# Probabilities as the stationary operand of probability x V, with a ones column in V, in a fused attention and SwiGLU kernel

## The chip, the cores and the metric

The kernel runs on one core of a Trainium2 chip. The metric is the device time of one execution in microseconds (us). Before the change it is 379.1 us (median of 4 runs, 378.8 to 379.4). In these runs the time is always 1.7 us more than the span from the first to the last instruction that a profile shows.

## The reference, cut to what matters

```python
B, H, S, D = 4, 8, 768, 64            # attention; d_ff = 1536, d_model = H * D = 512
scores = q @ k.T / sqrt(D)            # per batch and head
scores = where(mask, scores, -1e9)    # block mask of 32x32 blocks
attn = exp(scores - max);  attn = attn / (sum(attn) + 1e-9)
x = (attn @ v) with the heads side by side        # (B*S, 512)
xn = x / sqrt(mean(x * x) + 1e-6) * rms_g
out = (silu(xn @ w_gate) * (xn @ w_val)) @ w_out  # (3072, 512), float32
```

## The kernel before

The program counts in *units* of 384 tokens (half a batch; 8 of them) and in *head pairs* (4 per unit, 32 in all). A software pipeline has 192 steps; each step does the scores of one pair for 128 keys (two matmuls) and their exp on ScalarE. The probability x V of a pair, the norm of a unit and the feed-forward of the unit before are placed between the steps by a fixed list and a work queue. Scores come out with keys on partitions, so the probabilities `pt` are already laid out as either operand of the product with V.

Before the change V is the stationary operand and the probabilities stream through. The two heads of a pair use the two 64-column halves of the array at the same time (in the trace the second head's matmul starts 3 to 4 ns after the first's). The result has head and value dimension on partitions, as the feed-forward wants it. The row sums of the probabilities need matmuls of their own, in four 32-column parts of the array:

```python
def av(n, shared):
    ...
    for jt in range(NC):                       # NC = 6 blocks of 128 keys
        for e in range(2):                     # two heads
            nc.tensor.matmul(
                out=o_[64 * e:64 * e + 64, :],
                lhsT=vb[:, 2 * pr + e, jt * D:(jt + 1) * D],
                rhs=pt_[:, jt, e, :], start=(jt == 0), stop=(jt == NC - 1), ...)
    nc.vector.tensor_copy(out=osb[u][:, pr, :], in_=o_)
    nc.gpsimd.tensor_tensor(                   # squares for the norm
        out=o2s[u][:, pr, :], in0=osb[u][:, pr, :], in1=osb[u][:, pr, :], op=ALU.mult)

def zsum(n):                                   # row sums: 12 matmuls of 32 x 384
    ...
                    nc.tensor.matmul(
                        out=zwt[u][32 * c:32 * c + 32, :], lhsT=Ez[:, pr, :],
                        rhs=pt_[:, 2 * j2 + par, e, :], ...)
# norm_a ... norm_e (cut): sums and sums of squares are gathered by selection matmuls,
# turned by fp32 matmuls, combined on VectorE, turned back, and broadcast to 128
# partitions by matmuls; VectorE multiplies them into osb to make xn.
...
LAG = 13                                       # steps from a unit's scores to its feed-forward
    at(s1 + 1, 1.2, av, n, n >= 8)
    at(s1 + 1, 0.7, zsum, n)
    if pr == NP - 1:
        at(s1 + 4, 0.4, norm_a, u)  ...  at(s1 + 12, 0.35, norm_e, u, 1)
```

`at(step, cost, function, ...)` puts a function at a step; `s1` is the first step after a pair's scores.

The softmax here doesn't subtract the row's maximum and nothing guards it: scores larger than these inputs give would overflow.

Of the kernel before, what the change touches and what calls it, by code (L numbers as in the profile page):

```python
# [17 lines left out]
def kernel(  # L18
# [12 lines left out]
    nc = tc.nc  # L31
# [34 lines left out]
    qraw, kraw, vtiles = {}, {}, {}  # L66
# [8 lines left out]
    def load_v(b):  # L75
        vtiles[b] = vpool.tile([P, H, NC * D], BF16, name="vb", tag="vb")
        nc.gpsimd.dma_start(out=vtiles[b], in_=vv[b])
# [6 lines left out]
    gcol = const.tile([P, DM // P], FP32, name="gcol")  # L84
    nc.sync.dma_start(out=gcol, in_=moe_rms_g.rearrange("(c p) -> p c", p=P))
# [95 lines left out]
    for ic in range(2):  # L181
        qm = ps_a.tile([32, TG], FP32, name="qm", tag="zw" if ic else "acc")
        nc.tensor.matmul(
            out=qm, lhsT=Bneg[0:NB, :],
            rhs=Kindf[0:NB, ic * TG:(ic + 1) * TG], start=True, stop=True)
        nc.scalar.copy(
            out=Xm[:, 0:2, 0, ic * TG:(ic + 1) * TG],
            in_=qm.unsqueeze(1).to_broadcast([32, 2, TG]))

    def mask_rows(lo, hi):  # L190
# [7 lines left out]
    Ez = const.tile([P, NP, 32], BF16, name="Ez")  # L198
    nc.gpsimd.memset(Ez, 0.0)
    nc.gpsimd.affine_select(  # L200
        out=Ez, in_=Ez, compare_op=ALU.not_equal, fill=1.0,
        base=0, pattern=[[1, NP], [-1, 32]], channel_multiplier=0)
    Ew = const.tile([P, 32], BF16, name="Ew")
    nc.gpsimd.memset(Ew, 0.0)
    for e in range(2):
        nc.gpsimd.memset(Ew[64 * e:64 * e + 64, 16 + e:17 + e], 1.0)

    Sel = const.tile([P, 16], FP32, name="Sel")
    nc.gpsimd.memset(Sel, 0.0)
    for half in range(2):  # L210
        nc.gpsimd.affine_select(
            out=Sel[:, 0:8], in_=Sel[:, 0:8], compare_op=ALU.not_equal, fill=1.0,
            base=-32 * half, pattern=[[-1, NP], [-64, 2]], channel_multiplier=1)
    nc.gpsimd.affine_select(
        out=Sel[:, 8:16], in_=Sel[:, 8:16], compare_op=ALU.not_equal, fill=1.0,
        base=-16, pattern=[[-32, NP], [-1, 2]], channel_multiplier=1)

    SelB = const.tile([P, NP, 2, D], BF16, name="SelB")
    nc.gpsimd.memset(SelB, 0.0)
    for half in range(2):  # L220
        nc.gpsimd.affine_select(
            out=SelB, in_=SelB, compare_op=ALU.not_equal, fill=1.0,
            base=-32 * half, pattern=[[-2, NP], [-1, 2], [0, D]], channel_multiplier=1)
    FHL = [const.tile([P, NT, P], BF16, name=f"FHL{i}") for i in range(2)]
    for t in FHL:
        nc.gpsimd.memset(t, 0.0)
# [5 lines left out]
    ptiles, osb, zwt, xns, hps, o2s = {}, {}, {}, {}, {}, {}  # L232
# [16 lines left out]
    def av(n, shared):  # L249
        u, pr = divmod(n, NP)  # L250
        b = u // 2
        pt_, vb = ptiles[n], vtiles[b]
        if pr == 0:
            osb[u] = opool.tile([P, NP, TG], FP32, name="osb", tag="osb")
            o2s[u] = work.tile([P, NP, TG], BF16, name="o2", tag="o2")
            zwt[u] = ps_a.tile([P, 512], FP32, name="zw", tag="zw")[:, 0:TG]
        if shared:
            o_ = ps_s.tile([P, 2, 512], FP32, name="o_", tag="s")[:, 0, 0:TG]
        else:
            o_ = ps_a.tile([P, 512], FP32, name="oa", tag="acc")[:, 0:TG]  # L260
        for jt in range(NC):
            for e in range(2):
                nc.tensor.matmul(  # L263
                    out=o_[64 * e:64 * e + 64, :],
                    lhsT=vb[:, 2 * pr + e, jt * D:(jt + 1) * D],
                    rhs=pt_[:, jt, e, :], start=(jt == 0), stop=(jt == NC - 1),
                    skip_group_check=True)
        nc.vector.tensor_copy(out=osb[u][:, pr, :], in_=o_)  # L268
        nc.gpsimd.tensor_tensor(  # L269
            out=o2s[u][:, pr, :], in0=osb[u][:, pr, :], in1=osb[u][:, pr, :], op=ALU.mult)  # L270

    def zsum(n):
        u, pr = divmod(n, NP)
        pt_ = ptiles[n]
        for j2 in range(NC // 2):
            for e in range(2):
                for par in range(2):
                    c = 2 * e + par
                    nc.tensor.matmul(  # L279
                        out=zwt[u][32 * c:32 * c + 32, :], lhsT=Ez[:, pr, :],  # L280
                        rhs=pt_[:, 2 * j2 + par, e, :],
                        start=(pr == 0 and j2 == 0), stop=False, skip_group_check=True)

    nrm = {}

    def norm_a(u):
        for pr in range(NP):
            nc.tensor.matmul(
                out=zwt[u][32 * pr:32 * pr + 32, :], lhsT=Ew, rhs=o2s[u][:, pr, :],
                start=False, stop=True, skip_group_check=True)  # L290
        zs = work.tile([P, TG], FP32, name="zs", tag="zs")
        nc.vector.tensor_copy(out=zs, in_=zwt.pop(u))
        nrm[u] = zs

    def norm_b(u):
        zs = nrm[u]
        zt = ps_a.tile([P, NT, 16], FP32, name="zt", tag="zw")
        for t in range(NT):
            nc.tensor.matmul(
                out=zt[:, t, :], lhsT=zs[:, t * P:(t + 1) * P], rhs=Sel,  # L300
                start=True, stop=True)
        zc = work.tile([P, NT, 16], FP32, name="zc", tag="zc")
        nc.vector.tensor_copy(out=zc, in_=zt)
        rz = work.tile([P, NT, 8], FP32, name="rz", tag="rz")
        nc.vector.reciprocal(out=rz, in_=zc[:, :, 0:8])
        w1 = work.tile([P, NT, 8], FP32, name="w1", tag="w1")
        nc.vector.tensor_tensor(out=w1, in0=zc[:, :, 8:16], in1=rz, op=ALU.mult)
        nc.vector.tensor_tensor(out=w1, in0=w1, in1=rz, op=ALU.mult)
        ms = work.tile([P, NT], FP32, name="ms", tag="ms")
        nc.vector.reduce_sum(out=ms, in_=w1, axis=mybir.AxisListType.X)  # L310
        nc.vector.tensor_scalar(  # L311
            out=ms, in0=ms, scalar1=1.0 / DM, scalar2=1e-6, op0=ALU.mult, op1=ALU.add)
        rs = work.tile([P, NT], FP32, name="rs", tag="rs")
        nc.gpsimd.tensor_tensor(out=rs, in0=ms, in1=nhalf, op=ALU.pow)  # L314
        nrm[u] = (rz, rs)

    def norm_c(u):
        rz, rs = nrm[u]
        fx = work.tile([P, NT, 8], FP32, name="fx", tag="fx")
        nc.vector.tensor_tensor(  # L320
            out=fx, in0=rz, in1=rs.unsqueeze(2).to_broadcast([P, NT, 8]), op=ALU.mult)
        fh = FHL[u % 2]
        nc.vector.tensor_copy(out=fh[:, :, 0:8], in_=fx)
        nc.vector.tensor_tensor(
            out=fh[:, :, 32:40], in0=fx, in1=fh[:, :, 0:8], op=ALU.subtract)

    def norm_d(u):
# [85 lines left out]


    NSTEP = NU * NP * NC
    LAG = 13
    RESERVE = 5
    fixed = {}

# [109 lines left out]
```

## Time and profile before

| | before |
|---|---|
| time, median | 379.1 us |
| TensorE busy / granted clock | 93% / 0.996 |
| ScalarE / VectorE / GpSimd busy | 53% / 55% / 16% |
| first feed-forward matmul | at 52.4 us |
| row sums and probability x V, per pair | 0.60 + 1.10 us, and 0.09 on entering |

The page of the kernel before, part 1 (busy us, share of the span, instructions) and two lines of part 2 (40 slices of the span, each digit a share in tenths):

```profile
PE 352.9 (93%) x2730; PEld 187.9 (49%) x2730; DVE 210.1 (55%) x411; ACT 200.5 (53%) x302; POOL 60.9 (16%) x88
...
PE   2998889988899999999999999999999999999995
...
PEclk9999999999999999999999999999999999999999
```

TensorE is nearly full from the first tenth of the run on. The clock row holds only what was recorded: the first record of the trace is at 22.7 us, so its first 9s say nothing. The other engines have room. The waits of TensorE over the whole run (who waited for whom: us in total, times, longest) are short, and the two longest rows of the list, with one of the single waits, belong to the start or to a few spots:

```profile
PE tqk L165 <- DMA qb<-in_q_dram: 5.0, 1, 5.0
PE ft L332 <- DVE osb L268: 2.3, 3, 1.1
...
PE fb L350 <- ACT pt L246: 0.9, 1, 0.9
```

One head pair in the timeline of TensorE (start, busy us, line, output<-inputs, shape). Busy times of matmuls overlap, so cost is read from one start to the next start:

```profile
190.01 0.49 PE L242 MATMUL s__2404<-X 88*128 88x384 bf16 x2
190.43 1.17 PE L263 MATMUL o__2408<-pt,vb 128*64 128x384 bf16 x12
191.53 0.67 PE L279 MATMUL zw<-pt,Ez 128*32 128x384 bf16 x12
192.13 0.34 PE L242 MATMUL s__2435<-X 88*128 88x384 bf16 x1
```

Probability x V takes 191.53 - 190.43 = 1.10 us, the row sums 192.13 - 191.53 = 0.60 us. The score matmuls ahead of them fill 0.42 us where a pair of them elsewhere takes 0.33 (here 2 x 162 ns): about 0.09 us is lost on entering the 64-column tiling. The Trainium skill says in "TensorEngine Tiling (Array Packing)", Key Properties, that changing the tiling mode drains the array; the trace agrees with about 0.09 us, and the same 0.09 us stand at the other borders of a tiling (32-column sums, 64-column transposes).

### The profile page before, as it was taken

The page shows a single profiled execution, that of the slowest core. Times are in us where ns is not written, and L with a number is a line of the kernel's source. Part 1 is how long each engine was busy: PE and PEld are TensorE (multiplying, and loading weights), DVE is VectorE, ACT ScalarE, POOL GpSimd, SP SyncE. Part 2 cuts the span into 40 slices and gives each one's busy share as a digit, 9 for nine tenths or more (in the row PEclk, how much of TensorE's full clock was granted, in tenths as well). Part 3 has the DMA queues.
Part 4 walks back from the last instruction along what each step waited for, and adds up shares of the span by engine and source line. Part 5 has one row for each costly group of instructions (what it writes and reads, how often), then busy time and mean ns, then how long its engine had stood idle before and what let it go on. Part 6 is the DMA issues. An engine that isn't in the chain of part 4 may idle for free.

```text
span 379.9 us, 6604 instructions
## 1 busy us (share of the span) xinstructions
PE 352.9 (93%) x2730; PEld 187.9 (49%) x2730; DVE 210.1 (55%) x411; ACT 200.5 (53%) x302; POOL 60.9 (16%) x88
## 2 busy tenths in 40 slices
PE   2998889988899999999999999999999999999995
PEld 1443345554555555555555555555555455545552
DVE  5642355666646564665645655565444644676650
ACT  2658566665555555556555555556566566122221
POOL 8970110130010100020010100010000100000000
PEclk9999999999999999999999999999999999999999
DMA  5999970091060000091050000000000000000012
GB/s 70 179 210 207 205 130 2 2 148 19 2 101 11 28 29 2 28 151 45 29 83 29 29 0 29 30 15 14 28 30 0 29 0 29 28 29 28 29 39 99
DMA packets 20257, 20.86 MB, mean 55 GB/s; under 512 B 1284, under 2 KB 17156, under 8 KB 20228
## 3 DMA queue, kind: packets, MB, share of 16 engines
q0 software_dynamic: 16208, 14.16, 24.3%
q1 hardware_dynamic: 4020, 6.30, 4.4%
q8 instruction: 21, 0.34, 0.4%
q14 instruction: 8, 0.07, 0.1%
HBM read 28.31 MB, written 6.29 MB: 91 GB/s over the span
## 4 chain that ended last, share of the span: by engine, by line
PE 76%; DVE 10%; ACT 6%; issue 3%; DMA 2%; POOL 1%; POOLq 0%; DVEq 0%
PE yp L401 14%; PE gp L370 14%; PE vp L387 13%; PE zw L279 5%; ACT pt L246 3%; PE oa L263 3%; ACT th L374 2%; DVE uu L376 2%; DVE xn L355 2%; DVE X L171 2%; PE tqk L165 1%; DVE X L174 1%; DMA kb<-in_k_dram 1%; DMA out_dram<-yo 1%; PE vw L387 1%
## 5 line engine op out<-in xcount | busy, mean ns | idle before, releaser
L376 DVE SCALAR_TENSOR_TENSOR uu<-th,gp 128x384 bf16<-128x384 bf16 x90 | 49.8, 554 | 86.5 <-ACT th L374 86.0
L401 PE MATMUL yp<-wo,hp 128*128 128x512 bf16 x288 | 75.9, 379 | 0.0
L387 PE MATMUL vp<-xn,wv 128*128 128x384 bf16 x360 | 73.2, 325 | 1.3 <-DVE hp L390 1.3
L370 PE MATMUL gp<-xn,wg 128*128 128x384 bf16 x360 | 73.3, 326 | 1.1 <-DVE uu L376 1.1
L374 ACT ACTIVATE th<-gp 128x384 bf16<-128x384 f32 x90 | 44.0, 489 | 50.8 <-PE gp L370 50.8
L242 PEld LDWEIGHTS <-X 88*128 88x128 bf16 x384 | 35.1, 100 | 48.8 <-issue 19.9
L390 DVE TENSOR_TENSOR hp<-uu,vp 128x384 bf16<-128x384 bf16 x90 | 49.8, 553 | 15.9 <-PE vp L387 8.1
L370 PEld LDWEIGHTS <-wg 128*128 128x128 bf16 x384 | 36.6, 97 | 31.8 <-issue 3.3
L387 PEld LDWEIGHTS <-wv 128*128 128x128 bf16 x384 | 36.7, 98 | 26.8 <-issue 2.9
L401 PEld LDWEIGHTS <-hp 128*128 128x128 bf16 x288 | 27.8, 98 | 24.8 <-issue 0.4
L263 PEld LDWEIGHTS <-vb 128*64 128x64 bf16 x384 | 21.1, 112 | 19.1 <-issue 12.7
L174 DVE COPY X<-tqk 64x1536 bf16<-64x1536 bf16 x26 | 24.8, 954 | 5.2 <-PE tqk L165 4.9
L279 PE MATMUL zw<-pt,Ez 128*32 128x384 bf16 x384 | 22.1, 337 | 0.0
L355 DVE SCALAR_TENSOR_TENSOR xn<-osb,gcol,fb 128x384 bf16<-128x384 f32 x28 | 15.9, 609 | 1.7 <-PE fb L350 1.6
L314 POOL TENSOR_TENSOR rs<-ms,nhalf 128x3 f32<-128x3 f32 x8 | 6.9, 866 | 55.8 <-DVE ms L311 55.8
L410 DVE TENSOR_SCALAR yo<-yp 128x512 f32<-128x512 f32 x21 | 14.4, 686 | 0.2
L279 PEld LDWEIGHTS <-Ez 128*32 128x32 bf16 x384 | 7.4, 96 | 12.3 <-issue 10.7
L165 PE MATMUL tqk<-ident,qb 128*64 128x128 bf16 x156 | 7.2, 230 | 5.1 <-DMA qb<-in_q_dram 5.0
L165 PEld LDWEIGHTS <-qb 128*64 128x64 bf16 x192 | 6.7, 120 | 10.3 <-issue 5.3
L263 PE MATMUL oa<-pt,vb 128*64 128x384 bf16 x96 | 11.3, 379 | 0.0
L268 DVE COPY osb<-oa 128x384 f32<-128x384 f32 x8 | 4.5, 557 | 11.3 <-PE oa L263 11.2
L269 POOL TENSOR_TENSOR o_1613<-osb 128x384 bf16<-128x384 f32 x4 | 3.3, 826 | 30.3 <-DVE osb L268 30.3
(557 smaller groups left out, 461.7 us busy)
## 6 DMA issues: line engine op xcount, KB each, us to landing
out_dram<-yo SPq DMA_DIRECT2D x24, 256.0 KB, 2.0
vb<-in_v_dram POOLq DMA_DIRECT2D x4, 768.0 KB, 8.1
qb<-in_q_dram POOLq DMA_DIRECT2D x3, 768.0 KB, 7.4
kb<-in_k_dram POOLq DMA_DIRECT2D x3, 768.0 KB, 11.4
wg<-in_moe_w_gate_dram POOLq DMA_DIRECT2D x2, 768.0 KB, 11.7
wv<-in_moe_w_val_dram POOLq DMA_DIRECT2D x2, 768.0 KB, 14.1
wo<-in_moe_w_out_dram POOLq DMA_DIRECT2D x1, 1536.0 KB, 30.8
qb<-in_q_dram POOLq DMA_DIRECT2D x2, 192.0 KB, 3.6
```

The source lines that it names most:

```text
L165: nc.tensor.transpose(out=tt[i][64 * h:64 * h + 64, c * P:(c + 1) * P], in_=src[:, 2 * pr + h, c * D:(c + 1) * D], identity=ident)
L174: nc.vector.tensor_copy(out=X[0:D, sl, h], in_=t_[64 * h:64 * h + 64, :, 0:S])
L242: nc.tensor.matmul(out=s_[:, e, 0:TG], lhsT=X[0:D + NB, sl, e, 1, jt * P:(jt + 1) * P], rhs=X[0:D + NB, sl, e, 0, ic * TG:(ic + 1) * TG], ...
L263: nc.tensor.matmul(out=o_[64 * e:64 * e + 64, :], lhsT=vb[:, 2 * pr + e, jt * D:(jt + 1) * D], rhs=pt_[:, jt, e, :], start=(jt == 0), stop ...
L279: nc.tensor.matmul(out=zwt[u][32 * c:32 * c + 32, :], lhsT=Ez[:, pr, :], rhs=pt_[:, 2 * j2 + par, e, :], start=(pr == 0 and j2 == 0), stop ...
L355: nc.vector.scalar_tensor_tensor(out=xns[u][:, pr, :], in0=osb[u][:, pr, :], scalar=gcol[:, pr:pr + 1], in1=fb[i], op0=ALU.mult, op1=ALU.mult)
L370: nc.tensor.matmul(out=gp, lhsT=wg[:, c, f * P:(f + 1) * P], rhs=xns[u][:, c, :], start=(c == 0), stop=(c == NP - 1))
L374: nc.scalar.activation(out=th, in_=gp, func=AF.Tanh, scale=0.5)
L376: nc.vector.scalar_tensor_tensor(out=uu, in0=th, scalar=1.0, in1=gp, op0=ALU.add, op1=ALU.mult)
L387: nc.tensor.matmul(out=vp, lhsT=wv[:, c, f * P:(f + 1) * P], rhs=xns[u][:, c, :], start=(c == 0), stop=(c == NP - 1))
L390: nc.vector.tensor_tensor(out=hps[u][:, f, :], in0=uu, in1=vp, op=ALU.mult)
L401: nc.tensor.matmul(out=yp, lhsT=hps[u][:, f, t * P:(t + 1) * P], rhs=wo[:, f, :], start=(f == 0), stop=(f == NF - 1))
```

## The change

The operands are swapped: the probabilities are loaded as weights (128 keys x 128 queries), and V streams, 64 columns and a 65th of ones. The output has queries on partitions, and its 65th column is the row sum, so the separate sums go, and dividing is a reciprocal and a multiplication per partition. The norm now reduces along the free dimension (square with accumulation on ScalarE). As the feed-forward wants features on partitions, the normed rows are transposed on TensorE and copied by ScalarE out of PSUM, the memory that the kernel's matmuls write to. V is copied into a padded tile once per batch. The core of the diff:

```diff
-    for jt in range(NC):
+        for t in range(NT):                    # 3 blocks of 128 queries
             for e in range(2):
-                nc.tensor.matmul(
-                    out=o_[64 * e:64 * e + 64, :],
-                    lhsT=vb[:, 2 * pr + e, jt * D:(jt + 1) * D],
-                    rhs=pt_[:, jt, e, :], start=(jt == 0), stop=(jt == NC - 1), ...)
+                for jt in range(NC):
+                    nc.tensor.matmul(
+                        out=o_[:, t, e, :], lhsT=pt_[:, jt, e, t * P:(t + 1) * P],
+                        rhs=va[:, (2 * pr + e) * NC + jt, 0:D + 1],
+                        start=(jt == 0), stop=(jt == NC - 1))
+        nc.vector.reciprocal(out=rz, in_=o_[:, :, :, D])
+        nc.vector.tensor_tensor(out=xos[u][...], in0=o_[:, :, :, 0:D], in1=rz..., op=ALU.mult)
-    def zsum(n): ...                           # 12 row-sum matmuls a pair
     def norm_a(u):
+        for t in range(NT):
+            nc.scalar.activation(
+                out=sq, in_=xo[:, t, :], func=AF.Square, accum_out=ms[:, t:t + 1])
+    # norm_b: mean, power on GpSimd; norm_c: three multiplies of 128x512 on VectorE
+    def norm_d(u, lo, hi):
+        tr = ps_a.tile([P, 2, NP, P], BF16, name="tr", tag="o")   # the bank of o_ too
+        for t in range(lo, hi):
+            for c in range(NP):
+                nc.tensor.transpose(out=tr[:, t - lo, c, :], in_=xqs[u][...], identity=ident)
+        nc.scalar.copy(out=xns[u][...], in_=tr[:, 0:hi - lo])
...
-    LAG = 13
+    LAG = 9
+        at(s1 + 1, 1.3, av, n)
+            at(s1 + 2, 0.0, norm_a, u)
+            at(s1 + 4, 0.0, norm_b, u)
+            at(s1 + 5, 0.0, norm_c, u)
+            at(s1 + 6, 0.5, norm_d, u, 0, 2)
+            at(s1 + 7, 0.25, norm_d, u, 2, 3)
+    at(6, 0, pad_v, 0)
```

The transposes `tr` and the outputs `o_` have the same tag in a pool with one buffer (`ps_a`), so they share one bank.

More of the change, by code (lines that the diff above doesn't have):

```diff
@@ L64 @@
     vv = v.rearrange("b h (p c) d -> b p h (c d)", c=NC)
-    qraw, kraw, vtiles = {}, {}, {}
+    qraw, kraw, vraw = {}, {}, {}
+    vaug = [const.tile([P, H * NC, D + 2], BF16, name=f"vaug{i}") for i in range(2)]
+    for t in vaug:
+        nc.vector.memset(t[:, :, D:D + 1], 1.0)
     def load_qk(b, lo, hi):
@@ L75, in load_v, with pad_v @@
     def load_v(b):
-        vtiles[b] = vpool.tile([P, H, NC * D], BF16, name="vb", tag="vb")
-        nc.gpsimd.dma_start(out=vtiles[b], in_=vv[b])
+        vraw[b] = raw.tile([P, H, NC * D], BF16, name="vr", tag="vr", bufs=1)
+        nc.gpsimd.dma_start(out=vraw[b], in_=vv[b])
+    def pad_v(b):
+        va = vaug[b % 2]
+        vr = vraw.pop(b).rearrange("p h (c d) -> p (h c) d", d=D)
+        nc.vector.tensor_copy(out=va[:, :, 0:D], in_=vr)
     samp_i = const.tile([32, 2 * NRND], I32, name="samp_i")
@@ L83 @@
     nc.sync.dma_start(out=samp_i[0:NB, :], in_=s64)
-    gcol = const.tile([P, DM // P], FP32, name="gcol")
-    nc.sync.dma_start(out=gcol, in_=moe_rms_g.rearrange("(c p) -> p c", p=P))
+    gB = const.tile([P, DM], FP32, name="gB")
+    nc.sync.dma_start(out=gB, in_=moe_rms_g.unsqueeze(0).to_broadcast([P, DM]))
     load_qk(0, 0, 2)
@@ L181 @@
     for ic in range(2):
-        qm = ps_a.tile([32, TG], FP32, name="qm", tag="zw" if ic else "acc")
+        qm = ps_a.tile([32, TG], FP32, name="qm", tag="o" if ic else "acc")
         nc.tensor.matmul(
@@ L194, in mask_rows @@
             out=Xm[:, lo:hi, 0, :], in_=Xm[:, 0:1, 0, :].to_broadcast([32, hi - lo, S]))
-    Ez = const.tile([P, NP, 32], BF16, name="Ez")
-    nc.gpsimd.memset(Ez, 0.0)
-    nc.gpsimd.affine_select(
-        out=Ez, in_=Ez, compare_op=ALU.not_equal, fill=1.0,
-        base=0, pattern=[[1, NP], [-1, 32]], channel_multiplier=0)
-    Ew = const.tile([P, 32], BF16, name="Ew")
-    nc.gpsimd.memset(Ew, 0.0)
-    for e in range(2):
-        nc.gpsimd.memset(Ew[64 * e:64 * e + 64, 16 + e:17 + e], 1.0)
-    Sel = const.tile([P, 16], FP32, name="Sel")
-    nc.gpsimd.memset(Sel, 0.0)
-    for half in range(2):
-        nc.gpsimd.affine_select(
-            out=Sel[:, 0:8], in_=Sel[:, 0:8], compare_op=ALU.not_equal, fill=1.0,
-            base=-32 * half, pattern=[[-1, NP], [-64, 2]], channel_multiplier=1)
-    nc.gpsimd.affine_select(
-        out=Sel[:, 8:16], in_=Sel[:, 8:16], compare_op=ALU.not_equal, fill=1.0,
-        base=-16, pattern=[[-32, NP], [-1, 2]], channel_multiplier=1)
-    SelB = const.tile([P, NP, 2, D], BF16, name="SelB")
-    nc.gpsimd.memset(SelB, 0.0)
-    for half in range(2):
-        nc.gpsimd.affine_select(
-            out=SelB, in_=SelB, compare_op=ALU.not_equal, fill=1.0,
-            base=-32 * half, pattern=[[-2, NP], [-1, 2], [0, D]], channel_multiplier=1)
-    FHL = [const.tile([P, NT, P], BF16, name=f"FHL{i}") for i in range(2)]
-    for t in FHL:
-        nc.gpsimd.memset(t, 0.0)
     nhalf = const.tile([P, NT], FP32, name="nhalf")
@@ L230 @@
     load_w(1)
-    ptiles, osb, zwt, xns, hps, o2s = {}, {}, {}, {}, {}, {}
+    ptiles, xos, xns, hps, rss, xqs = {}, {}, {}, {}, {}, {}
     def qk_exp(n, jt):
@@ L247, in qk_exp, with av @@
             out=ptiles[n][:, jt, :, :], in_=s_[:, :, 0:TG], func=AF.Exp, scale=SCALE)
-    def av(n, shared):
+    def av(n):
         u, pr = divmod(n, NP)
-        b = u // 2
-        pt_, vb = ptiles[n], vtiles[b]
+        pt_, va = ptiles.pop(n), vaug[(u // 2) % 2]
         if pr == 0:
-            osb[u] = opool.tile([P, NP, TG], FP32, name="osb", tag="osb")
-            o2s[u] = work.tile([P, NP, TG], BF16, name="o2", tag="o2")
-            zwt[u] = ps_a.tile([P, 512], FP32, name="zw", tag="zw")[:, 0:TG]
-        if shared:
-            o_ = ps_s.tile([P, 2, 512], FP32, name="o_", tag="s")[:, 0, 0:TG]
-        else:
-            o_ = ps_a.tile([P, 512], FP32, name="oa", tag="acc")[:, 0:TG]
-        for jt in range(NC):
-            for e in range(2):
-                nc.tensor.matmul(
-                    out=o_[64 * e:64 * e + 64, :],
-                    lhsT=vb[:, 2 * pr + e, jt * D:(jt + 1) * D],
-                    rhs=pt_[:, jt, e, :], start=(jt == 0), stop=(jt == NC - 1),
-                    skip_group_check=True)
-        nc.vector.tensor_copy(out=osb[u][:, pr, :], in_=o_)
-        nc.gpsimd.tensor_tensor(
-            out=o2s[u][:, pr, :], in0=osb[u][:, pr, :], in1=osb[u][:, pr, :], op=ALU.mult)
@@ L272, in zsum @@
-    def zsum(n):
-        u, pr = divmod(n, NP)
-        pt_ = ptiles[n]
-        for j2 in range(NC // 2):
-            for e in range(2):
-                for par in range(2):
-                    c = 2 * e + par
-                    nc.tensor.matmul(
-                        out=zwt[u][32 * c:32 * c + 32, :], lhsT=Ez[:, pr, :],
-                        rhs=pt_[:, 2 * j2 + par, e, :],
-                        start=(pr == 0 and j2 == 0), stop=False, skip_group_check=True)
-    nrm = {}
-    def norm_a(u):
-        for pr in range(NP):
-            nc.tensor.matmul(
-                out=zwt[u][32 * pr:32 * pr + 32, :], lhsT=Ew, rhs=o2s[u][:, pr, :],
-                start=False, stop=True, skip_group_check=True)
-        zs = work.tile([P, TG], FP32, name="zs", tag="zs")
-        nc.vector.tensor_copy(out=zs, in_=zwt.pop(u))
-        nrm[u] = zs
@@ L295, in norm_b @@
-    def norm_b(u):
-        zs = nrm[u]
-        zt = ps_a.tile([P, NT, 16], FP32, name="zt", tag="zw")
-        for t in range(NT):
-            nc.tensor.matmul(
-                out=zt[:, t, :], lhsT=zs[:, t * P:(t + 1) * P], rhs=Sel,
-                start=True, stop=True)
-        zc = work.tile([P, NT, 16], FP32, name="zc", tag="zc")
-        nc.vector.tensor_copy(out=zc, in_=zt)
-        rz = work.tile([P, NT, 8], FP32, name="rz", tag="rz")
-        nc.vector.reciprocal(out=rz, in_=zc[:, :, 0:8])
-        w1 = work.tile([P, NT, 8], FP32, name="w1", tag="w1")
-        nc.vector.tensor_tensor(out=w1, in0=zc[:, :, 8:16], in1=rz, op=ALU.mult)
-        nc.vector.tensor_tensor(out=w1, in0=w1, in1=rz, op=ALU.mult)
-        ms = work.tile([P, NT], FP32, name="ms", tag="ms")
-        nc.vector.reduce_sum(out=ms, in_=w1, axis=mybir.AxisListType.X)
-        nc.vector.tensor_scalar(
-            out=ms, in0=ms, scalar1=1.0 / DM, scalar2=1e-6, op0=ALU.mult, op1=ALU.add)
-        rs = work.tile([P, NT], FP32, name="rs", tag="rs")
-        nc.gpsimd.tensor_tensor(out=rs, in0=ms, in1=nhalf, op=ALU.pow)
-        nrm[u] = (rz, rs)
@@ L317, in norm_c @@
-    def norm_c(u):
-        rz, rs = nrm[u]
-        fx = work.tile([P, NT, 8], FP32, name="fx", tag="fx")
-        nc.vector.tensor_tensor(
-            out=fx, in0=rz, in1=rs.unsqueeze(2).to_broadcast([P, NT, 8]), op=ALU.mult)
-        fh = FHL[u % 2]
-        nc.vector.tensor_copy(out=fh[:, :, 0:8], in_=fx)
-        nc.vector.tensor_tensor(
-            out=fh[:, :, 32:40], in0=fx, in1=fh[:, :, 0:8], op=ALU.subtract)
-    def norm_d(u):
-        fh = FHL[u % 2]
-        ft = (ps_f.tile([P, TG], FP32, name="ft0", tag="vp") if u == 0
-              else ps_s.tile([P, TG], FP32, name="ft", tag="s"))
-        for t in range(NT):
-            nc.tensor.matmul(
-                out=ft[:, t * P:(t + 1) * P], lhsT=fh[:, t, :], rhs=ident,
-                start=True, stop=True)
-        fs = work.tile([P, TG], BF16, name="fs", tag="fs")
-        nc.scalar.copy(out=fs, in_=ft)
-        nrm[u] = fs
@@ L339, in norm_e @@
-    def norm_e(u, half):
-        fs = nrm[u]
-        if half == 0:
-            xns[u] = opool.tile([P, NP, TG], BF16, name="xn", tag="xn")
-        if u == 0:
-            fb = [ps_f.tile([P, TG], FP32, name="fb0", tag=t) for t in ("gp", "vp")]
-        else:
-            fb_ = ps_s.tile([P, 2, 512], FP32, name="fb", tag="s")
-            fb = [fb_[:, i, 0:TG] for i in range(2)]
-        for i in range(2):
-            pr = 2 * half + i
-            nc.tensor.matmul(
-                out=fb[i], lhsT=SelB[:, pr].rearrange("p e d -> p (e d)"),
-                rhs=fs, start=True, stop=True)
-        for i in range(2):
-            pr = 2 * half + i
-            nc.vector.scalar_tensor_tensor(
-                out=xns[u][:, pr, :], in0=osb[u][:, pr, :], scalar=gcol[:, pr:pr + 1],
-                in1=fb[i], op0=ALU.mult, op1=ALU.mult)
+            xos[u] = opool.tile([P, NT, H, D], FP32, name="xo", tag="xo")
@@ new lines, in av @@
+        o_ = ps_a.tile([P, 512], FP32, name="o_", tag="o")[:, 0:NT * 2 * (D + 1)].rearrange(
+            "p (t e d) -> p t e d", t=NT, e=2)
+        for t in range(NT):
+            for e in range(2):
+                for jt in range(NC):
+                    nc.tensor.matmul(
+                        out=o_[:, t, e, :], lhsT=pt_[:, jt, e, t * P:(t + 1) * P],
+                        rhs=va[:, (2 * pr + e) * NC + jt, 0:D + 1],
+                        start=(jt == 0), stop=(jt == NC - 1))
+        rz = work.tile([P, NT, 2], FP32, name="rz", tag="rz")
@@ new lines, in av @@
+        nc.vector.reciprocal(out=rz, in_=o_[:, :, :, D])
+        nc.vector.tensor_tensor(
+            out=xos[u][:, :, 2 * pr:2 * pr + 2, :], in0=o_[:, :, :, 0:D],
+            in1=rz.unsqueeze(3).to_broadcast([P, NT, 2, D]), op=ALU.mult)
+    def norm_a(u):
+        xo = xos[u].rearrange("p t h d -> p t (h d)")
+        ms = work.tile([P, NT], FP32, name="ms", tag="ms")
+        for t in range(NT):
+            sq = work.tile([P, DM], BF16, name="sq", tag="sq")
+            nc.scalar.activation(
+                out=sq, in_=xo[:, t, :], func=AF.Square, accum_out=ms[:, t:t + 1])
+        rss[u] = ms
@@ new lines, in norm_b, with norm_c @@
+    def norm_b(u):
+        ms = rss[u]
+        m2 = work.tile([P, NT], FP32, name="m2", tag="m2")
+        nc.vector.tensor_scalar(
+            out=m2, in0=ms, scalar1=1.0 / DM, scalar2=1e-6, op0=ALU.mult, op1=ALU.add)
+        rs = work.tile([P, NT], FP32, name="rs", tag="rs")
+        nc.gpsimd.tensor_tensor(out=rs, in0=m2, in1=nhalf, op=ALU.pow)
+        rss[u] = rs
+    def norm_c(u):
+        xo = xos[u].rearrange("p t h d -> p t (h d)")
+        xqs[u] = work.tile([P, NT, DM], BF16, name="xq", tag="xq")
+        for t in range(NT):
+            nc.vector.scalar_tensor_tensor(
+                out=xqs[u][:, t, :], in0=xo[:, t, :], scalar=rss[u][:, t:t + 1],
+                in1=gB, op0=ALU.mult, op1=ALU.mult)
@@ new lines, in norm_d @@
+    def norm_d(u, lo, hi):
+        if lo == 0:
+            xns[u] = opool.tile([P, NP, TG], BF16, name="xn", tag="xn")
+        tr = ps_a.tile([P, 2, NP, P], BF16, name="tr", tag="o")
+        for t in range(lo, hi):
+            for c in range(NP):
+                nc.tensor.transpose(
+                    out=tr[:, t - lo, c, :], in_=xqs[u][:, t, c * P:(c + 1) * P], identity=ident)
+        nc.scalar.copy(
+            out=xns[u][:, :, lo * P:hi * P].rearrange("p c (t q) -> p t c q", t=hi - lo),
+            in_=tr[:, 0:hi - lo])
@@ L397, in ff_y @@
             yst[(u, t)] = ps_a.tile(
-                [P, DM], FP32, name="yp", tag="zw" if u == NU - 1 and t != 1 else "acc")
+                [P, DM], FP32, name="yp", tag="o" if u == NU - 1 and t != 1 else "acc")
         yp = yst[(u, t)]
@@ L425 @@
         s1 = 6 * (n + 1)
-        at(s1 + 1, 1.2, av, n, n >= 8)
-        at(s1 + 1, 0.7, zsum, n)
+        at(s1 + 1, 1.3, av, n)
         if pr == NP - 1:
-            at(s1 + 4, 0.4, norm_a, u)
-            at(s1 + 6, 0.5, norm_b, u)
-            at(s1 + 7, 0.0, norm_c, u)
-            at(s1 + 8, 0.3, norm_d, u)
-            at(s1 + 10, 0.35, norm_e, u, 0)
-            at(s1 + 12, 0.35, norm_e, u, 1)
+            at(s1 + 2, 0.0, norm_a, u)
[3 more added lines that the diff above has]
+            at(s1 + 7, 0.25, norm_d, u, 2, 3)
     for pr in range(1, NP):
@@ L443 @@
         at(6 * (8 * (b - 1) + (1 if b == 1 else 4)), 0, load_v, b)
+    at(6, 0, pad_v, 0)
+    for b in range(1, B):
+        at(6 * 8 * b + 2, 0, pad_v, b)
     at(7, 0, load_wo)
@@ L477 @@
             since += cost
-            if fn in (norm_d, norm_e):
+            if fn is norm_d:
                 gap = 0.9
```

## The prediction

> What bounds the kernel now. TensorE: busy 93% (page, part 1), granted clock 0.996, 76% of the chain that ended last. The first feed-forward matmul starts at 52.4 us (timeline); until then the exps of ScalarE (0.81 us each) and the VectorE copies set the pace. From 60 to 330 us TensorE shows only 8 us of waiting, so its work is the time.
>
> What goes, per head pair (timeline, 190.4 to 192.1 us): probability x V 1.10 us, row-sum matmuls 0.60, and 0.09 of waiting on entering the 64-column tiling: 1.79 us, 32 times = 57 us. (The Trainium skill, "TensorEngine Tiling (Array Packing)", Key Properties: a change of tiling mode drains the array; the trace agrees, 0.09 us at each border.) Also gone per unit of 384 tokens: the norm's matmuls, 14.6 us over 8 units, plus 0.2 us of drains each.
>
> What comes. 36 matmuls of 65 columns per pair, each with its own 128-column weight load. The cost of such a load/matmul couple is the main unknown. 65 columns are 27 ns at the trace's 2.4 columns per ns. A full bf16 load took 96 ns from end to end, the same as a 32-column one (112 to 120 for 64, 191 for fp32), so its streaming part I estimate at about 27 ns (the skill, "TensorE: Matmul & The Clock Gate", Fast Weight Load, says four chunks in parallel; the equal durations agree). In the three factor transposes (128 columns) couples followed at 55 ns, so loads hide behind matmuls. Estimate: 35 ns a couple (28 to 55), 1.26 us a pair, 0.53 saved; about 26 pairs lie in the TensorE-bound part: 14 us. Twelve transposes per unit at 55 ns against 1.8 us before: 1.3 us saved, 9.5 us over seven units. Removed work on the critical path: 23 us.
>
> What it gives back. ScalarE gets three squares per unit (about 0.6 us each, by the 128x512 output copy) and two PSUM copies (estimates 1.0 and 0.6 us, from 0.84 ns per element): 3.4 us a unit, busy to about 225 us.  All outputs and transposes share one PSUM bank: the second transpose group waits for the first copy, and the next probability x V follows it at once and waits for the second copy, behind an exp. By hand: about 0.6 + 1.2 us, 1.2 us from the squares delaying exp and tanh, 0.5 us from three 0.7 us VectorE multiplies; 3.5 us a unit against 1.3 us before. Loss: 15 us, of which I expect some to be absorbed, so 11 to 15.
>
> Start: V's padding stands behind the mask copies on VectorE, which end at 20.1 us, so the first probability x V moves from 17.6 to about 21.5 us. The lag shrinks from 13 to 9 steps; together the first feed-forward matmul stays at 49 to 53 us: no gain, within 2 us.
>
> Sum: 379.3 - 23 + 12 = about 368 us; range 353 to 384.
> Chances: faster 0.57, same 0.35, slower 0.08.
>
> What would show it: probability x V slots of 1.1 to 1.5 us; TensorE busy falling to about 325 us, but its waits growing, on ScalarE's copy of the transposes (second transpose group, next probability x V) and in the score matmuls after the squares; ScalarE up by about 23 us; the first feed-forward matmul near 51 us.
>
> What would make it wrong: a couple at 55 ns or more (load not hidden) makes it no faster, near 380; a couple at 28 ns and absorbed waits give 355.

## The result and the profile after

The changed kernel takes 372.9 us (median of 4 runs, 372.4 to 373.6), the kernel before 379.1. The ratio is 0.9834 (95% interval 0.981 to 0.986): 1.7% faster, which is inside 2%. A ratio here and below is the mean time of one kernel's fast runs over that of the other's of the same rounds, so it is not quite the ratio of the medians.

The page of the changed kernel, the same lines:

```profile
PE 326.6 (88%) x3074; PEld 197.0 (53%) x3074; DVE 203.0 (55%) x369; ACT 221.8 (60%) x358; POOL 27.4 (7%) x42
...
PE   2768689977989789988999889998999799989995
...
PEclk9999859999999999999999999999999999999999
```

TensorE works 26 us less, but its row now has 7s and 8s all along. A head pair in the timeline of TensorE:

```profile
183.37 0.49 PE L221 MATMUL s__2456<-X 88*128 88x384 bf16 x2
183.69 1.31 PE L238 MATMUL o__2460<-vaug,pt 128*128 128x65 bf16 x36
184.85 0.49 PE L221 MATMUL s__2500<-X 88*128 88x384 bf16 x2
```

The 36 matmuls take 1.16 us, 32 ns for each couple of a weight load and a matmul (median of the 32 pairs: 1.148 us), and the score matmuls before them take their 0.32 us again: no drain. This replaces 1.79 us. The waits of TensorE:

```profile
PE gp L297 <- DVE uu L303: 5.6, 9, 1.4
PE tr L280 <- DVE xq L270: 3.7, 11, 0.6
...
PE s__1071 L221 <- ACT pt L225: 1.7, 1, 1.7
PE s__1685 L221 <- ACT pt L225: 1.4, 1, 1.4
PE o__1138 L238 <- ACT xn L282: 1.2, 1, 1.2
...
PE o__2911 L238 <- ACT xn L282: 0.9, 1, 0.9
```

The waits of `tr` for `xq` and of `o__` for `xn` are new; those of `gp` for `uu` were 1.1 us in all before, and after 60 us no single wait of a score matmul for an exp was over 0.5. The wait of `o__` for `xn` stands there in seven of the eight units. Two places in the timeline show where they come from. First the squares, in the fourth unit (`sq` is the square, `th` and `uu` are steps of the feed-forward, bracketed figures are idle time and its end):

```profile
163.86 0.62 ACT L253 ACTIVATE sq<-xo 128x512 bf16<-128x512 f32 x1
...
164.38 0.19 ACT L253 ACTIVATION_READ_ACCUMULATOR sq<-xo 128x1 f32 x1
...
165.60 0.19 ACT L253 ACTIVATION_READ_ACCUMULATOR sq<-xo 128x1 f32 x1
165.70 0.47 ACT L301 ACTIVATE th<-gp 128x384 bf16<-128x384 f32 x1
...
166.20 0.55 DVE L303 SCALAR_TENSOR_TENSOR uu<-th,gp 128x384 bf16<-128x384 bf16 x1 [1.72 <-ACT th L301]
166.81 0.32 PE L297 MATMUL gp<-xn,wg 128*128 128x384 bf16 x1 [1.41 <-DVE uu L303]
```

The three squares and their accumulator reads hold ScalarE from 163.86 to 165.7 us. A tanh stands behind them, VectorE needs it, and TensorE needs VectorE to free the one bank of `gp`: TensorE waits 1.41 us. In the other units the waits of TensorE just after the squares, for a tanh or an exp, are 0.4 to 2.0 us; the eight together are 9.9 us. Then the shared bank:

```profile
171.34 0.40 PE L280 MATMUL tr<-ident,xq 128*128 128x128 bf16 x4 [0.27 <-DVE xq L270]
...
171.77 1.01 ACT L282 COPY xn<-tr 128x1024 bf16<-128x1024 bf16 x1 [0.27 <-PE tr L280]
...
172.84 0.38 PE L280 MATMUL tr<-ident,xq 128*128 128x128 bf16 x4
...
173.46 0.58 ACT L282 COPY xn<-tr 128x512 bf16<-128x512 bf16 x1
174.09 1.30 PE L238 MATMUL o__2333<-vaug,pt 128*128 128x65 bf16 x36 [0.87 <-ACT xn L282]
```

The second transposes, a copy on ScalarE behind an exp, and probability x V follow each other through one bank, and TensorE stands still for the copy.

An account of TensorE's time, summed from start to next start: each kind of matmul is counted at its undisturbed spacing (162 ns for 384 columns, 215 for 512, 32 for a new couple, and so on; drains of the old tiling, 3.8 us, counted as work), and the rest is waiting. It is good to about 1 us.

| us, profiled executions | before | after | difference |
|---|---|---|---|
| to the first feed-forward matmul | 52.4 | 52.5 | +0.1 |
| after it: work of TensorE | 304.6 | 281.9 | -22.7 |
| after it: all else | 18.7 | 32.2 | +13.5 |

The profiled execution of the kernel before was 2 to 3 us longer than its timed ones (span 379.9 us; the spans of the timed ones of these rounds are 377 to 378), so this difference, 9 us, is larger than the 6.2 us of the medians. The record shows what they go with: in the rounds of the experiments the kernel before took 380.6 to 381.8 us in the 12 executions with a granted clock of 0.995 or 0.996, and 377.6 to 379.8 us in the 16 with 0.997 or more. The profiled one had 0.996, with a clock of 0.5 from 36.4 to 39.8 us.

### The profile page after: what moved, and what is told of

Same layout as the page of the kernel before. It is cut to its first block, busy times and chain, and to the rows that moved or that the text cites. A ratio compares the mean times of both kernels' runs of the same rounds, so it can differ in the third digit from the quotient of the medians.

```text
span 371.2 us, 7228 instructions
## 1 busy us (share of the span) xinstructions
PE 326.6 (88%) x3074; PEld 197.0 (53%) x3074; DVE 203.0 (55%) x369; ACT 221.8 (60%) x358; POOL 27.4 (7%) x42
## 4 chain that ended last, share of the span: by engine, by line
PE 68%; ACT 15%; DVE 11%; DMA 2%; issue 2%; POOL 1%; DVEq 0%; POOLq 0%
PE gp L297 13%; PE yp L328 13%; PE vp L314 12%; ACT pt L225 6%; ACT sq L253 4%; ACT xn L282 3%; DVE xq L270 3%; DVE uu L303 2%; ACT th L301 2%; DVE X L179 2%; DVE X L182 2%; DMA kb<-in_k_dram 1%; PE tqk L173 1%; DMA out_dram<-yo 1%; PE gw L297 1%
## 5 line engine op out<-in xcount | busy, mean ns | idle before, releaser
L221 PEld LDWEIGHTS <-X 88*128 88x128 bf16 x384 | 36.0, 101 | 43.0 <-issue 13.9
L238 PEld LDWEIGHTS <-pt 128*128 128x128 bf16 x1152 | 42.5, 100 | 14.0 <-issue 10.8
L263 POOL TENSOR_TENSOR rs<-m,nhalf 128x3 f32<-128x3 f32 x8 | 6.9, 865 | 291.5 <-DVE m L260 291.5
L270 DVE SCALAR_TENSOR_TENSOR xq<-xo,rs,gB 128x512 bf16<-128x512 f32 x24 | 16.6, 747 | 1.6 <-POOL rs L263 1.6
L253 ACT ACTIVATE sq<-xo 128x512 bf16<-128x512 f32 x24 | 14.7, 618 | 2.1 <-DVE xo L244 2.1
L282 ACT COPY xn<-tr 128x1024 bf16<-128x1024 bf16 (+1 forms) x16 | 12.8, 798 | 4.3 <-PE tr L280 4.2
L280 PE MATMUL tr<-ident,xq 128*128 128x128 bf16 x96 | 10.1, 231 | 5.0 <-DVE xq L270 3.7
L280 PEld LDWEIGHTS <-xq 128*128 128x128 bf16 x96 | 6.4, 102 | 12.0 <-DVE xq L270 8.5
L301 ACT ACTIVATE th<-gw 128x384 bf16<-128x384 f32 x6 | 2.9, 490 | 8.8 <-PE gw L297 8.8
(529 smaller groups left out, 409.9 us busy)
```

The source lines that it names most:

```text
L221: nc.tensor.matmul(out=s_[:, e, 0:TG], lhsT=X[0:D + NB, sl, e, 1, jt * P:(jt + 1) * P], rhs=X[0:D + NB, sl, e, 0, ic * TG:(ic + 1) * TG], ...
L238: nc.tensor.matmul(out=o_[:, t, e, :], lhsT=pt_[:, jt, e, t * P:(t + 1) * P], rhs=va[:, (2 * pr + e) * NC + jt, 0:D + 1], start=(jt == 0), ...
L253: nc.scalar.activation(out=sq, in_=xo[:, t, :], func=AF.Square, accum_out=ms[:, t:t + 1])
L270: nc.vector.scalar_tensor_tensor(out=xqs[u][:, t, :], in0=xo[:, t, :], scalar=rss[u][:, t:t + 1], in1=gB, op0=ALU.mult, op1=ALU.mult)
L282: nc.scalar.copy(out=xns[u][:, :, lo * P:hi * P].rearrange("p c (t q) -> p t c q", t=hi - lo), in_=tr[:, 0:hi - lo])
L301: nc.scalar.activation(out=th, in_=gp, func=AF.Tanh, scale=0.5)
```

## The experiments

The theory (A): the work removed is real and is on the critical path, and the 13 us come back as waits that are made by the *order* of ScalarE's queue and of the users of one bank. Rivals: (B) the waits are only where slack shows, and go elsewhere when one is removed; (C) ScalarE has become the limit; (D) ScalarE's 21 us of extra work cost this much wherever they stand; and there are questions about the couple's cost, the start and the clock. All ratios are against the kernel before, of the same rounds (the rounds ran on different chips); the changed kernel has 0.9834. It did not run again in these rounds, so a step of 1 or 2 us against it is not settled by a ratio or by a median alone.

**The squares taken away.** The edit:

```diff
-        for t in range(NT):
-            nc.scalar.activation(out=sq, in_=xo[:, t, :], func=AF.Square, accum_out=ms[:, t:t + 1])
+        # cut: norm_b takes this one sum for all three blocks
+        nc.scalar.activation(out=sq[:, 0:64], in_=xo[:, 0, 0:64], func=AF.Square, accum_out=ms[:, 0:1])
```

> Changed kernel, but ScalarE computes one square of 64 elements per unit instead of three of 512 (wrong result on purpose). The squares and their accumulator reads took 1.85 us in one block per unit. Theory A (the block holds back exps and tanhs, and TensorE then waits for them): the waits of 1.4 to 2 us seen after the squares in most units go, about 8 us less than the changed kernel, ratio to the kernel before about 0.962. Rival B (TensorE's own work sets the time and these waits are hidden or merely move): at most 2 us less, ratio 0.978 or more.

Measured: 363.2 us, ratio 0.958 (0.954 to 0.962), so about 9.7 us less than the changed kernel. The waits of `gp` for `uu` fall from 5.6 to 0.6 us in all, and no wait of a score matmul for an exp is over 0.6 us; 2.1 us of the gain lie before the first feed-forward matmul (50.4 instead of 52.5 us), 8 after it:

```profile
PE gp L296 <- DVE uu L302: 0.6, 3, 0.2
```

The squares in one block cost about 10 us, although ScalarE stands at 60%. Theory A holds for them; this run alone does not tell order from amount.

**The second transposes one step later.**

```diff
-            at(s1 + 7, 0.25, norm_d, u, 2, 3)
+            at(s1 + 8, 0.25, norm_d, u, 2, 3)
```

> Changed kernel, second transpose group one step later, after the next probability x V. Theory A (the shared bank makes probability x V wait 0.9 to 1.2 us for ScalarE's second copy in each unit): those waits go, some of it comes back as a wait of the transposes; 4 to 7 us less than the changed kernel, ratio 0.965 to 0.973. Rival B (waits merely move): within 2 us of the changed kernel, ratio 0.978 to 0.989.

Measured: 371.0 us, ratio 0.978 (0.974 to 0.982): 2 us less, just inside the band of the rival, and the interval overlaps that of the changed kernel. Its waits of TensorE say why:

```profile
PE gp L297 <- DVE uu L303: 5.6, 9, 1.4
PE tr L280 <- DVE xq L270: 3.7, 11, 0.6
PE tr L280 <- DVE xo L244: 3.6, 7, 0.6
```

The wait of probability x V for the copy is gone; in its place the transposes, now right behind probability x V, wait for VectorE to read it from the same bank (third line, not there before). One neighbour was exchanged for another. Here rival B was right.

**The gain vector loaded later.** The change loads `rms_g` broadcast to 128 partitions; in the trace the first q tile reached TensorE at 6.4 us instead of 5.0.

```diff
-    nc.sync.dma_start(out=gB, in_=moe_rms_g...to_broadcast([P, DM]))     # before the first q, k load
+    nc.gpsimd.dma_start(out=gB, in_=moe_rms_g...to_broadcast([P, DM]))   # after the batch-0 loads
```

> Changed kernel, the broadcast load of the gain vector issued after the q, k, v loads of the first batch instead of before them. Theory: that load delayed the first q tile (first transposes at 6.4 us, against 5.0 before), so the start moves up by 1.4 us and the whole by 1 to 1.5 us, ratio about 0.980. Rival: the first q tile is late for another reason; no change.

Measured: 372.0 us, ratio 0.981 (0.977 to 0.985); the first transposes start at 4.9 us again. The load is what delayed the start, by 1.5 us. About 1 us of it arrives at the end, but the interval holds the ratio of the changed kernel too, so the size is not settled.

**Probability x V done twice.**

```diff
+                for rep in range(2):
                     for jt in range(NC):
                         nc.tensor.matmul(...)      # the 36 matmuls of a pair, start=(jt == 0) each time
```

> Changed kernel with the 36 probability x V matmuls of every head pair done twice (same result). A pair took 1.16 us in the changed kernel. Theory A (a load and matmul couple costs 32 ns and TensorE's work is the time outside the waits): 32 more ns per extra couple, 1.15 us x 27 to 32 pairs, so 28 to 37 us longer, ratio about 1.07. Rival C (TensorE is no longer what bounds, ScalarE's queue is): the extra work falls into waits, less than 20 us longer, ratio below 1.04.

Measured: 409.9 us, ratio 1.080 (1.076 to 1.086): 37 us more for 1152 more couples, 32 ns each. The whole of the added work on TensorE is paid in time (6.8 us of it before the first feed-forward matmul), even with the waits that it has now. Rival C falls for added work; that work saved in these matmuls is saved in time too fits the narrower couples below.

**Spread squares, separated bank users, an earlier start.** With the same amount of work, only the order is changed:

```diff
-            at(s1 + 2, 0.0, norm_a, u)            # three squares in one block
-            at(s1 + 4, 0.0, norm_b, u)
-            at(s1 + 5, 0.0, norm_c, u)
-            at(s1 + 6, 0.5, norm_d, u, 0, 2)
-            at(s1 + 7, 0.25, norm_d, u, 2, 3)
+            for t in range(NT):
+                at(s1 + 2 + t, 0.0, norm_a, u, t) # one square a step
+            at(s1 + 5, 0.0, norm_b, u)
+            at(s1 + 6, 0.0, norm_c, u)
+            at(s1 + 8, 0.5, norm_d, u, 0, 2)
+            at(s1 + 10, 0.25, norm_d, u, 2, 3)
-    LAG = 9
+    LAG = 11
+    # and the later gain load, and the first padding of V at step 4, ahead of the large mask copies
```

> Changed kernel, correct result: the three squares one per step instead of in one block, the two transpose groups two and four steps after the last norm step so that no two users of the shared bank follow each other, lag 11, the gain load after the first loads, the first padding before the large mask copies. Theory A (the give-back is waits made by the order of ScalarE's and the bank's users, not by the amount of work): most of the 9 us after the start and 2 us of the start come back, 372.9 to about 359, ratio 0.943 to 0.955. Rival D (ScalarE's extra 21 us of work cost this wherever they stand): at most 3 us less, ratio 0.975 or more.

Measured: 358.3, 359.1 and 360.8 us, ratio 0.948 (0.942 to 0.954). Rival D falls: ScalarE does the same work, and 13 us are gone, about 2 of them by the edits of the start (see the parts below). A fourth execution, the profiled one, took 1797 us; see the last section. So the kernel was run again:

> The same kernel as c1_spread, again, because its profile fell in an execution of 1797 us in which every matmul ran at about a sixth of its speed. Theory A: 358 to 361 us as in its three other runs, ratio 0.948 within 0.006; in the profile TensorE loses less than 14 us after the first feed-forward matmul (the changed kernel: 32 us against the ideal slots), and no wait of probability x V for ScalarE's copy is left.

Measured: 361.9 us median (358.7 to 362.3), ratio 0.949 (0.943 to 0.954), as before. Of the waits for ScalarE's copy one of 0.4 us is left, of a feed-forward matmul, and the waits for `uu` fell from 5.6 to 1.5 us in all. No probability x V waits for a copy. But the account's rest after the first feed-forward matmul was 23 us, not the under 14 that was expected. One new wait leads the list of TensorE's waits:

```profile
PE tr L280 <- DVE xo L244: 7.0, 7, 1.6
```

It is the neighbour of the second experiment again: the first transposes stand one step behind probability x V, in its bank. So the edit had not done what was expected of it, that no two users of the bank follow each other.

**The parts of it.** Only the transposes moved (and the lag):

> Changed kernel with only the transpose groups moved (to two and four steps after the norm step, lag 11), the squares in one block as they were, the start as it was. Theory A, split: the bank's share of the give-back is 4 to 6 us, ratio 0.967 to 0.973; the block of squares keeps costing the rest.

Measured: 370.1 us, ratio 0.973 (0.970 to 0.976). All of the reordering, without the two edits of the start:

> As c1_spread without its two edits of the start (gain load and padding where the changed kernel has them). Theory A, split: the spread squares give another 5 to 7 us over d2_transposes_only, and the start edits are worth 2 to 4 us, so ratio 0.953 to 0.960. If the start edits are worth nothing (rival: the stretch before the feed-forward is paced by ScalarE whatever its beginning), the ratio is that of c1_spread, 0.948.

Measured: 362.9 us, ratio 0.955 (0.951 to 0.959). The first is at the edge of its forecast: in its trace the waits of `gp` for `uu` are 8.7 us instead of 5.6, and the first transposes wait 4.4 us for `xo`. In steps of the ratio times 379 us: moving the transposes gives about 4 us (2.8 by the medians), spreading the squares a further 7, the start edits about 2 (their intervals overlap, so this last step is not settled; in the traces the first feed-forward matmul starts at 51.2 instead of 53.5 us). The second step is the clean one: both kernels have the lag of 11. The first one has the larger lag in it, and no run changes the lag alone, so how much of the 4 us is the lag's stays open.

**Idle matmuls against the clock.** The trace of the changed kernel has a granted clock of 0.5 from 43.6 to 53.8 us; before, it was at 1 from 39.8 us on.

```diff
+        if 14 <= step < 33:
+            for _ in range(2):
+                nc.tensor.matmul(out=wm, lhsT=X[...], rhs=X[...], start=True, stop=True)  # 384 columns, unused
```

> Changed kernel plus two idle matmuls of 384 columns per step from step 14 to 32, into a bank that nobody uses yet. In the changed kernel the granted clock is 0.5 from 43.6 to 53.8 us, in the kernel before only until about 40 us. Theory E (TensorE, with less work, waits so much at the start that its clock drops, and the work from there on runs at half speed): the clock stays at 1, the first feed-forward matmul comes 3 to 4 us earlier, ratio 0.972 to 0.976. Rival F (that stretch is paced by ScalarE anyway): within 1 us of the changed kernel, ratio 0.981 to 0.986.

Measured: 373.0 us, ratio 0.985 (0.979 to 0.991). The stretch at half clock shrank to 45.8 to 49.2 us, yet the first feed-forward matmul came at 52.9 us, not earlier. The result fits rival F, the stretch being paced by ScalarE. It is not clean: the added matmuls cost up to 6 us of TensorE's time in it, and the score matmul after the first squares came 1 us later. So either the lower clock did not cost the 3 to 4 us that I had expected, or the remedy cost as much.

**Narrower couples.** 30 of 36 matmuls with 33 columns (wrong on purpose, one look):

```diff
-                        rhs=va[:, (2 * pr + e) * NC + jt, 0:D + 1],
+                        rhs=va[:, (2 * pr + e) * NC + jt, 0:w],   # w = 33, and 65 for the last jt; out has 0:w too
```

> Changed kernel, 30 of the 36 probability x V matmuls of a pair with 33 columns instead of 65 (wrong result on purpose). Theory G (a couple costs the streaming of its weight load, about 27 to 32 ns, whatever the columns): about 32 ns a couple stay, 1.15 us a pair. Rival H (the 65 columns, 27 ns, and a fixed part set it): the narrow couples fall to 25 ns or less, a pair to 0.95 us or less.

Measured: the narrow couples follow at 25 to 26 ns and a pair takes 0.945 us; one run of 365.4 us. So at 65 columns the columns set the pace (27 ns at 2.4 columns per ns, and some 5 ns whose cause is open; the 65-column couples left in this run take 29 to 30 ns), not the load of 128 weights, which streams in 25 to 26 ns or less. The one run is 7.5 us below the median of the changed kernel, and 32 pairs are 6.5 us shorter; its state is unknown, so this only fits that the saving arrives. Theory G falls. The 25 ns agree with the floor of about 25 ns from start to start that the Trainium skill gives in "TensorE: Matmul & The Clock Gate", section "Wait — 56ns, not 53.3ns?".

**The kernel before with a third of its row sums**:

```diff
-        for j2 in range(NC // 2):
+        for j2 in range(1):
```

> The kernel before with only 4 of the 12 row-sum matmuls of each head pair (wrong result on purpose), probability x V as it was. Theory I (the row sums, 0.60 us a pair, are what the change saves in this part; the swap of operands alone saves almost nothing, 1.19 against 1.16 us): 0.32 to 0.36 us a pair less, 8 to 10 us in all, ratio 0.974 to 0.979. Rival J (the sums hide behind other engines' waits): under 4 us, ratio above 0.989.

Measured: 371.9 us, ratio 0.981 (0.976 to 0.987). The sums of a pair now take 0.28 instead of 0.60 us, 10 us over all pairs, and 7 us of it arrive:

```profile
187.30 0.35 PE L279 MATMUL zw<-pt,Ez 128*32 128x384 bf16 x4
187.58 0.50 PE L242 MATMUL s__2283<-X 88*128 88x384 bf16 x2
```

The gain is smaller than the forecast (the ratio lies above its band), whose edge lies inside the interval, and well above the rival: row sums were on the critical path, and dropping two thirds of them alone gives as much as the whole change did. Probability x V itself was not made cheaper to speak of (1.19 us with its drain before, 1.16 after; both are spacings in the traces).

**One more step between the users of the bank.**

```diff
-            at(s1 + 8, 0.5, norm_d, u, 0, 2)
-            at(s1 + 10, 0.25, norm_d, u, 2, 3)
+            at(s1 + 9, 0.5, norm_d, u, 0, 2)
+            at(s1 + 11, 0.25, norm_d, u, 2, 3)
-    LAG = 11
+    LAG = 12
```

> As d1_spread_again with the two transpose groups one step later each and lag 12. What is left in d1_spread_again after the start is a wait of the first transpose group for VectorE's read of the probability x V just before it, 7.0 us in seven units. Theory A carried on: with one more step between them 4 to 7 us of it go, 354 to 358 us, ratio 0.932 to 0.941. Rival: the later end of the norm and the larger lag give the same back at the start and at the end, ratio 0.945 or more.

Measured: 351.0 us (350.4 to 352.0), correct, ratio 0.924 (0.919 to 0.930). This version beats both kernels, and by more than expected. Its page and its longest remaining wait for `xo`:

```profile
PE 322.0 (92%) x3042; PEld 197.8 (57%) x3074; DVE 202.7 (58%) x369; ACT 220.5 (63%) x358; POOL 29.0 (8%) x43
...
PE   2897689989899999999999999999999999899994
```

```profile
PE tr L280 <- DVE xo L244: 0.6, 2, 0.4
```

The busy row of TensorE is back to 9s, ScalarE still does its 220 us, and the bank's wait fell from 7.0 to 0.6 us. (The trace lacks 32 records of matmuls, so its busy time is a few us too low.) In the account the rest after the first feed-forward matmul is 15 us, less than the 19 of the kernel before, at 281 us of work. That explains 8 of the 9 to 11 us (by the ratios or the medians) that it gained over the version with one step less; 2 more lie in the start, where the first feed-forward matmul came at 48.9 instead of 51.2 us. The clock has a part in this: the version with one step less ran at granted clocks of 0.971 to 0.989, this one at 0.983 to 0.994, and their executions at 0.989 and 0.988 took 358.7 and 350.4 us, 8.3 us apart. From its first clock record to 57 us the trace of the former has a clock of 0.5 for 20.5 us, this one for 10.2. Why that is so was not tested, and the lag grew by one here too.

## Why the prediction was right, and where it was off

The prediction was 368 us, range 353 to 384; the measured time is 372.9. Of the three classes it gave "faster by over 2%" 0.57 and "within 2%" 0.35; the second came true. The range is wide enough to hold the kernel before itself, so that the time lies in it says little; the terms say more.

- *The couple of load and matmul, 35 ns:* 32 ns were measured, and doubling them cost 32 ns each in time. The estimate from the two durations (27 ns of columns, a full bf16 load as short as a 32-column one) came close; that the couple is bound by its columns was left open, and the narrow couples showed it.
- *Work removed on the critical path, 23 us:* the account gives 22.7. Part of this agreement is luck: 15.5 us are of probability x V with its row sums and its drains (26 pairs of 1.79 us after that point before, 27 of 1.148 after; forecast 14) and so about 7 of the norm (forecast 9.5). The source is the row sums and the norm's matmuls; probability x V itself takes about as long as before.
- *The start, no gain within 2 us, first feed-forward matmul near 51 us:* 52.5 us. The first probability x V moved from 17.6 to 22.1 us behind the mask copies and the padding, as told. Two things were not foreseen: the 1.4 us by which the broadcast gain load held back the first q tile, and the stretch at half clock.
- *The give-back, "Loss: 15 us, of which I expect some to be absorbed, so 11 to 15", 12 in the sum:* this is the term that was mis-sized, a little: 13.5 us in the account, inside its own 11 to 15. The named waits were right in kind and near in size. The second copy costs probability x V 0.7 to 1.2 us a unit (forecast 1.2). The squares delay exp and tanh: "1.2 us from the squares" a unit is 9.6 us for eight units, the waits after them are 9.9 us, and the first experiment took 9.7 us away with them. The multiplies of VectorE cost 3.7 us over the run (`tr` for `xq`, forecast 0.5 a unit). The second transposes start 0.28 us later than undisturbed behind the first copy (forecast 0.6). That most of it was lost to the order, and could be had back, was not foreseen.
- *ScalarE up by 23 us, TensorE busy about 325:* measured 21.3 us more and 326.6.
- What remains of 368 against 372.9: with 22.7 us of work saved and 13.5 given back, the account gives 9 us, and the medians give 6.2. The 2 to 3 us between them are the profiled execution of the kernel before, which had the lower clock and was longer than its timed ones.

So the gain of the change was real and most of it was lost to order: three short ScalarE instructions in one block ahead of a tanh, and a PSUM bank handed from user to user without a step between them. With the same work in another order, a larger lag and two small edits of the start, the change is worth 7.6%, not 1.7%. (The order of the kernel before was not tuned again in the same way.)

## What to carry to other kernels

When an engine that is full is relieved, the work that moves to others must also find its place in their queues: here a block of 1.85 us on a 60% busy engine cost the full engine 1.2 us a unit on average (0.4 to 2.0), because the exp or a one-buffer chain (tanh, multiply, next matmul) stood behind it, and the same three instructions one per step gave 7 us of that back over the run. Users of one PSUM bank needed here a step of other work between each release and the next use: with it the wait fell from 7.0 to 0.6 us. Moving one of them by one place only exchanges the neighbour that is waited for, so move the group and look at the list of waits again. A ones column makes a row sum nearly free when the probabilities are stationary (a 65th column in a couple of 32 ns). The swap is what makes room for it, but it is the dropped sums and the norm's matmuls, not a cheaper product, that saved time.

## What the Trainium skill lacked or had wrong

- "TensorE: Matmul & The Clock Gate", Back-to-back issue gap: it gives a sustained 81 ns per matmul of 128 columns and 131 ns of 512 for streams with weight loads. Here 128-column couples (the transposes) followed at 55 ns and 512-column ones at 215 ns, each with its own load; that is by the columns, as the 56 and 216 ns that the page gives for isolated matmuls. 65-column couples followed at 32 ns and 33-column ones at 25 to 26 ns.
- The same page, Weight-path perf modes: it gives a measured gain of about 2 for the fast weight load. The 25 to 26 ns couples with 128-column bf16 loads mean that a load streams in at most that time. By the 107 ns that its formula P / 1.2 (section LDWEIGHTS) gives for 128 columns this is, as an estimate, a factor of about 4, which the page has as theory for fp8 only.
- "TensorEngine Tiling (Array Packing)", Key Properties: the drain on a mode change has no size there or on another page. Here it was about 0.09 us at each border.
- "ScalarE: Activation LUTs": it says that an activation can give an accumulator output, not that this is a second instruction. Here each one (ACTIVATION_READ_ACCUMULATOR) is on record with 0.19 us, and the squares of 0.62 us followed at 0.61 us from start to start: each read begins 0.1 us before its square ends, and the next square 0.1 us before the read ends.
- "TensorE: Matmul & The Clock Gate", HAM oscillation, and its rule of no idle gaps over about 3.4 us: in the changed kernel the clock fell to 0.5 at 43.6 us with no single wait of TensorE longer than 2.04 us in that stretch, only low use (three pairs of score matmuls between 40.4 and 43.6 us). What threshold of use it is was not measured.
- No page has a whole execution slowed like this: one of them took 1797 us. In it most matmuls of 384 columns followed at 0.87 to 1.05 us instead of 0.16, with the usual durations on VectorE and ScalarE (`uu` 554 ns, `th` 490). The run lists its clock as 1.0, but its trace holds no record of the clock at all, so this says nothing of it. It was one execution of one run, counted as slow, and its cause is open.
